# Chunked attention and a gated feed-forward on one core: first q through two hardware queues, moved groups from pair 6, paced loads, alternating moves, annealed orders

## The chip, the cores and the metric

One core of a Trainium2 chip runs the whole kernel. The metric is the device time of one execution in microseconds (us). The profiled execution has a span, from first to last instruction, that is 1.9 us shorter than the median time (251.2 and 249.3 before; the kernel before was timed once more beside the changed one, hence 251.4 below). A KB in the views is 1024 bytes; MB and GB/s are of 1000.

## The reference, cut to what matters

```python
# q, k, v: (8 batches, 8 heads, 576 tokens, 64); attention inside chunks of 64 tokens
scores = scale * q_c @ k_c.T ; attn = softmax(scores) ; out = attn @ v_c
x = out.transpose(0, 2, 1, 3).reshape(4608, 512)
a = x @ w1 ; b = x @ w2              # 512 -> 1024
h = a * b @ w3                       # 1024 -> 1024
return h @ w_out                     # 1024 -> 512, float32
```

The kernel multiplies w3 and w_out once (64 matmuls) and so needs 448 + 288 + 64 matmuls of 512 columns and 256 of 256 columns besides attention.

## The kernel before

The tokens are 18 "pairs" of 256 tokens, two to a group. One string gives the order of all steps; each engine executes its share of them strictly in that order. The letters:

- q, k, v: loads from memory with a cast to bf16, issued by POOL; i, o, h: loads of weights.
- T: VectorE transposes q or k of a pair (from the tile qk to qkT). S: scores, TensorE. E: exp, ScalarE. P: probabilities times v, TensorE. N: normalise, VectorE. X: transpose of the result, VectorE.
- A, B: x @ w1 and x @ w2, TensorE. C: copy of the first out of PSUM, ScalarE. M: product, VectorE. V, W, Z: w3 @ w_out. O, Y, Q: output matmul, copy, store.
- G, H: moves, of q and k (G, from qkT to qkm) and of the normalised result (H, from xm to xt). As the kernel lays its data out, the transpose leaves blocks of 32 partitions, so for early pairs scores are made with 32 contraction rows (64 matmuls a pair, the form 32*64 in the views). For "moved" pairs, DMAs from SBUF to SBUF (the memory on the chip that the engines read) put two blocks side by side first and 32 matmuls (64*64) do.
- D: matmuls of zeros whose result is not used. New in the change, R: a half of the first q, loaded as f32 by a hardware queue (SyncE's or ScalarE's); K: its cast to bf16, ScalarE.

```python
def load(dst, src):
    return inorder(nc.gpsimd.dma_start(dst, src))

vbuf = [consts.tile([P, 2, H, VW], bf, name=f"vbuf{i}") for i in range(6)]

def do_G(g, a):                       # moves of q and k of group g, 4 of 8
    if a == 0:
        qkm_t[g] = asb.tile([P, 2, 2, 2, H, CH], bf, tag="qkm", bufs=2, name="qkm")
    for i in (2 * a, 2 * a + 1):
        for e in range(2):
            move(qkm_t[g][blk[2 * a + e], i % 2], qkT_t[g][blk[i], e])

def do_S(p, hh=None):
    ...
        if p < 8:                     # 64 matmuls, 32 rows each
            ...
        else:                         # 32 matmuls, 64 rows each, from qkm
            ...

def do_M(p, j):
    if g not in ab_t:
        ab_t[g] = msb.tile([P, FO, GT], bf, tag="ab", bufs=3, name="ab")
    ...
# (cut: the other steps, and the order string)
```

The softmax here doesn't subtract the row's maximum and nothing guards it: scores larger than these inputs give would overflow.

## Time and profile before

| | before |
|---|---|
| median time | 251.2 us |
| span | 249.3 us |
| TensorE work at full rate (ledger of the prediction) | 217.8 us |
| lost until TensorE is dense (28.2 us) | 20.9 us |
| lost between there and the last matmul | 5.6 us |
| after the last matmul | 5.0 us |

In this profile, idle time counts only on the engine that sets the end. Here that is TensorE: it is full from 28 us on. So I read every other engine, and every transfer, by one question: does it make TensorE wait. The prediction below shows the lines.

### The profile page before, as it was taken

What the parts mean: (1) busy time and instruction counts of PE and PEld (TensorE: products, weight loads), DVE (VectorE), ACT (ScalarE), POOL (GpSimd) and SP (SyncE); (2) the same over time, 40 slices, a digit from 0 to 9 for tenths busy, and PEclk for the clock granted to TensorE, in tenths of its full rate; (3) what the DMA queues carried; (4) which work ended last, traced back from release to release, by engine and by line L of the source; (5) the groups of instructions that cost most, each with busy time, mean ns of one, the idle gap of its engine ahead of it and who ended that gap; (6) DMA issues with size and microseconds to landing.
All of it is one profiled execution on the core that took longest, in us unless ns stands there. A gap on an engine that the chain in (4) does not pass through costs nothing.

```text
span 249.3 us, 6372 instructions
## 1 busy us (share of the span) xinstructions
PE 226.9 (91%) x2740; PEld 122.0 (49%) x2760; DVE 154.5 (62%) x236; ACT 83.4 (33%) x116; POOL 86.9 (35%) x116
## 2 busy tenths in 40 slices
PE   3328899999999999999999999999999999999992
PEld 2225688874455445444444444444444444444441
DVE  2566965899879588999998798918440331233000
ACT  2110324332343333535335325262332332331322
POOL 8977854486997254573660000000000000000000
PEclk9999999999999999999999999999999999999998
DMA  7999999999999999999999974635502200400334
GB/s 67 145 165 182 193 185 201 196 174 172 155 169 209 221 225 249 177 209 193 204 194 235 271 128 99 147 76 199 151 3 84 84 0 9 162 0 1 139 116 168
DMA packets 93660, 37.12 MB, mean 149 GB/s; under 512 B 77120, under 2 KB 86592, under 8 KB 93632
## 3 DMA queue, kind: packets, MB, share of 16 engines
q0 software_dynamic: 84736, 19.41, 84.6%
q1 hardware_dynamic: 8896, 17.31, 24.0%
q8 instruction: 22, 0.36, 0.6%
q14 instruction: 6, 0.05, 0.1%
HBM read 38.80 MB, written 9.44 MB: 194 GB/s over the span
## 4 chain that ended last, share of the span: by engine, by line
PE 73%; DMA 17%; POOL 3%; DVE 2%; issue 1%; ACT 1%; SPq 0%; DVEq 0%; ACTq 0%; POOLq 0%
PE ab_ps L93 41%; PE o_ps L93 22%; DMA out_dram<-o_sb 6%; DMA w<-in_moe_w_dram 6%; PE w_ps L93 6%; DMA qkm<-qkT 5%; PE s_ps L93 3%; PE pv L93 2%; POOL qk L96 2%; DVE qkT L177 1%; POOL vbuf L96 1%; ACT e L209 0%; DVE ab L321 0%; POOL w L96 0%; ACT a_sb L306 0%
## 5 line engine op out<-in xcount | busy, mean ns | idle before, releaser
L93 PE MATMUL ab_ps<-xt,w 128*128 128x512 bf16 (+1 forms) x697 | 130.0, 343 | 1.1 <-DMA w<-in_moe_w_dram 0.5
L93 PEld LDWEIGHTS <-w 128*128 128x128 bf16 x704 | 67.8, 99 | 55.6 <-DMA w<-in_moe_w_dram 0.9
L321 DVE TENSOR_TENSOR ab<-a_sb,ab_ps 128x512 bf16<-128x512 f32 x72 | 48.9, 679 | 49.3 <-ACT a_sb L306 49.2
L306 ACT COPY a_sb<-ab_ps 128x512 f32<-128x512 f32 x72 | 42.2, 585 | 87.9 <-PE ab_ps L93 85.9
L93 PE MATMUL o_ps<-w3o,ab 128*128 128x512 bf16 (+1 forms) x285 | 63.3, 373 | 0.6
L177 DVE STREAM_TRANSPOSE qkT<-qk 128x1024 bf16<-128x1024 bf16 (+1 forms) x40 | 45.6, 1178 | 11.0 <-DMA qk<-in_q_dram 8.3
L93 PEld LDWEIGHTS <-ab 128*128 128x128 bf16 x296 | 28.5, 98 | 32.2
L96 POOL DMA_DIRECT2D vbuf<-in_v_dram x40 | 33.8, 854 | 14.6 <-DMA qk<-in_q_dram 6.4
L351 ACT COPY o_sb<-o_ps 128x1024 f32<-128x1024 f32 x17 | 17.2, 1012 | 42.8 <-PE o_ps L93 38.8
L239 DVE TENSOR_TENSOR xn<-pv,rc 128x512 bf16<-128x512 f32 x36 | 24.9, 692 | 1.2
L96 POOL DMA_DIRECT2D qk<-in_k_dram x26 | 20.2, 782 | 10.0 <-DMA vbuf<-in_v_dram 7.3
L96 POOL DMA_DIRECT2D qk<-in_q_dram x26 | 20.3, 788 | 8.2 <-DMA qk<-in_k_dram 2.3
L209 ACT ACTIVATE e<-s_ps 128x1024 bf16<-128x1024 f32 (+1 forms) x18 | 17.1, 978 | 8.9 <-PE s_ps L93 8.7
L93 PE MATMUL pv<-vbuf,e 64*32 64x65 bf16 (+1 forms) x832 | 11.0, 200 | 4.5 <-DMA vbuf<-in_v_dram 3.3
L93 PE MATMUL w_ps<-wo,w3T 128*128 128x512 bf16 x62 | 14.0, 379 | 0.1
L93 PEld LDWEIGHTS <-e 64*32 64x32 bf16 (+1 forms) x832 | 8.3, 99 | 11.5 <-issue 6.6
L236 DVE RECIPROCAL rc<-pv 128x8 f32<-128x8 f32 x36 | 6.9, 192 | 11.3 <-PE pv L93 11.2
L96 POOL DMA_DIRECT2D w<-in_moe_w_dram x16 | 11.1, 696 | 7.4 <-DMA wo<-in_moe_w_out_dram 3.4
L259 DVE STREAM_TRANSPOSE xm<-xn 128x512 bf16<-128x512 bf16 x20 | 13.6, 697 | 0.2
L251 DVE STREAM_TRANSPOSE xt<-xn 128x512 bf16<-128x512 bf16 x16 | 11.3, 707 | 0.4
L93 PEld LDWEIGHTS <-qkT 32*64 32x64 bf16 x512 | 5.8, 116 | 11.2 <-DVE qkT L177 9.2
L344 DVE COPY o_sb<-o_ps 128x256 f32<-128x256 f32 x1 | 0.4, 424 | 16.0 <-PE o_ps L93 16.0
(19 smaller groups left out, 45.4 us busy)
## 6 DMA issues: line engine op xcount, KB each, us to landing
out_dram<-o_sb SPq DMA_DIRECT2D x17, 512.0 KB, 2.9
qkm<-qkT SPq DMA_DIRECT2D x40, 128.0 KB, 7.2
vbuf<-in_v_dram POOLq DMA_DIRECT2D x32, 128.0 KB, 8.7
w<-in_moe_w_dram POOLq DMA_DIRECT2D x16, 256.0 KB, 10.0
qk<-in_q_dram POOLq DMA_DIRECT2D x10, 256.0 KB, 8.3
qk<-in_k_dram POOLq DMA_DIRECT2D x10, 256.0 KB, 10.1
xt<-xm SPq DMA_DIRECT2D x40, 64.0 KB, 3.0
qk<-in_q_dram POOLq DMA_DIRECT2D x8, 128.0 KB, 5.1
```

The lines of the kernel that those rows point to most:

```text
L93: return inorder(nc.tensor.matmul(*a, **kw))
L96: return inorder(nc.gpsimd.dma_start(dst, src))
L177: inorder(nc.vector.transpose(qkT_t[g][:, :, p % 2, s, heads(h)].rearrange("p e h (y t) -> p h t e y", t=2), qk_t[p][:, s, heads(h)].rearr ...
L209: inorder(nc.scalar.activation(e_t[p][:, :, heads(hh)], s_t[p][:].rearrange("p u (h q) -> p u h q", q=CH)[:, :, heads(hh)], Exp, scale=sca ...
L236: inorder(nc.vector.reciprocal(rc[:], pv[:, :, :, D:W]))
L239: inorder(nc.vector.tensor_mul(xn_t[p][:, u], pv[:, :, :, 0:D], rc.to_broadcast([P, 2, 4, D])))
L251: inorder(nc.vector.transpose(new_xt(g)[:].rearrange("p (o t) -> p o t", o=KO)[:, :, t0:t0 + UT] .rearrange("p o (m y) -> p m o y", y=BL), ...
L259: inorder(nc.vector.transpose(xm_t[g][:, u, :, m].rearrange("p o (c y) -> p c o y", y=BL), xn_t[p][:].rearrange("p u r m d -> p (u r) m d" ...
L306: inorder(nc.scalar.copy(a_t[p, j][:], ps_t[p, j][:, 0, :]))
L321: inorder(nc.vector.tensor_mul(o, view(a_t.pop((p, j))[:]), view(ps_t.pop((p, j))[:, 1, :])))
L344: inorder(copy(o_sb[:, u, n0:n1], t[:, 0, 0:n1 - n0]))
L351: inorder(nc.scalar.copy(o_sb[:], ps_t.pop(p)[:]))
```

## The change

Its intent: start TensorE earlier, save small matmuls in two more pairs, keep the loads from crowding the moves (three in flight), spread the moves over the blocks, and a new order of all steps found by annealing (a random search).

```diff
-q0.0 k0.0 q0.1 k0.1 v0 q1.0 q1.1 k1.0 k1.1 i0 v1 q2 k2 i1 v2 i2 i3 q3 k3 v3 o h0 h1 q4 k4 v4
-D0.0.32.64 T0.0.0 T0.1.0 T0.0.1 S0.0 T0.1.1 q5 k5 v5 E0.0 S0.1 ...
+R0 R1 k0 v0 q1 k1 v1 i1 i0 q2 k2 v2 i2 i3 q3 k3 v3 h0 o h1 q4 k4 v4 K0 K1 T0.0 T0.1 q5 k5 v5 S0 E0
+T1.0 D2.0.0.1 P0 N0.0 T1.1 ...
 # (cut: the rest of both orders; the new one has G3, H3 and ends Y15 Q15 Y16 Q16 O17)
+    def load(dst, src, paced=False):
+        if paced:
+            inorder(nc.gpsimd.tensor_copy(tick[0:1], last[-3]))
+        ins = inorder(nc.gpsimd.dma_start(dst, src))
 ...
+def do_R(h):
+    raw_t[h] = msb.tile([P, HH, 2 * D], f32, tag="o_sb", name="raw")
+    inorder((nc.sync, nc.scalar)[h].dma_start(raw_t[h][:], q[0, heads(h), ...]))
+def do_K(h):
+    inorder(nc.scalar.copy(qk_t[0][:, 0, heads(h)], raw_t[h][:]))
 # q, k and v loads pass paced = (p >= 6)
-        for i in (2 * a, 2 * a + 1):
-            for e in range(2):
-                move(qkm_t[g][blk[2 * a + e], i % 2], qkT_t[g][blk[i], e])
+        for i in (0, 2, 1, 3):
+            e = (i + a) % 2
+            move(qkm_t[g][blk[i // 2 * 2 + e], i % 2], qkT_t[g][blk[i], e])
 # the same in do_H; p < 8 becomes p < 6 in S, P, X, M; vbuf 6 -> 7 tiles, ab 3 -> 4
```

The copy into `tick` reads one element of the load three before. POOL works in order, so the next load is not issued until that one has landed.

More of the change, by code (lines that the diff above doesn't have):

```diff
@@ L9 @@
 ORDER = """
-q0.0 k0.0 q0.1 k0.1 v0 q1.0 q1.1 k1.0 k1.1 i0 v1 q2 k2 i1 v2 i2 i3 q3 k3 v3 o h0 h1 q4 k4 v4
-D0.0.32.64 T0.0.0 T0.1.0 T0.0.1 S0.0 T0.1.1 q5 k5 v5 E0.0 S0.1 E0.1 P0.0 P0.1 T1.0.0 N0.0 T1.1.0
-T1.0.1 S1.0 T1.1.1 q6 k6 v6 E1.0 X0.0 S1.1 N0.1 X0.1 P1.0 E1.1 T2.0 A0.0 T2.1 q7 k7 B0.0 C0.0 P1.1
-v7 M0.0 A0.1 N1.0 B0.1 C0.1 X1.0 S2 N1.1 E2 M0.1 X1.1 P2 A1.0 N2.0 B1.0 X2.0 C1.0 A1.1 N2.1 B1.1
-M1.0 C1.1 X2.1 A2.0 M1.1 B2.0 C2.0 A2.1 M2.0 B2.1 T3.0 C2.1 A0.2 M2.1 B0.2 C0.2 T3.1 q8 k8 v8 A1.2
@@ L15 @@
-M0.2 B1.2 C1.2 S3 M1.2 A2.2 E3 B2.2 C2.2 P3 M2.2 A0.3 N3.0 B0.3 X3.0 C0.3 A1.3 N3.1 B1.3 M0.3 C1.3
-X3.1 A2.3 M1.3 B2.3 C2.3 A3.0 M2.3 B3.0 V0 C3.0 A3.1 M3.0 B3.1 V1 C3.1 A3.2 M3.1 B3.2 C3.2 V2 A3.3
-M3.2 B3.3 C3.3 V3 W0 M3.3 T4.0 W1 Z0 V4 V5 T4.1 q9 k9 v9 W2 Z1 V6 V7 T5.0 S4 Z2 W3 T5.1 q10 k10 E4
-T6.0 T6.1 P4 v10 q11 k11 Z3 S5 N4.0 O0 E5 X4.0 N4.1 X4.1 T7.0 O1 T7.1 Y0 Q0 T8.0 P5 v11 q12 k12 Y1
-S6 T8.1 O2 Q1 E6 N5.0 X5.0 N5.1 X5.1 O3 T9.0 T9.1 Y2 G4.0 P6 v12 q13 k13 A4.0 N6.0 B4.0 G4.1 Y3 X6.0
@@ L20 @@
-N6.1 C4.0 A4.1 X6.1 B4.1 C4.1 M4.0 Q2 S7 Q3 M4.1 A4.2 E7 T10.0 B4.2 C4.2 T10.1 P7 v13 q14 k14 A4.3
-M4.2 B4.3 N7.0 C4.3 A4.4 X7.0 M4.3 B4.4 C4.4 N7.1 A4.5 M4.4 B4.5 C4.5 X7.1 S8 M4.5 S9 E8 A4.6 T11.0
-B4.6 E9 T11.1 P8 v14 q15 k15 C4.6 A4.7 M4.6 G5.0 B4.7 C4.7 N8.0 A6.0 M4.7 B6.0 N8.1 C6.0 G5.1 A6.1
-X8.0 B6.1 M6.0 C6.1 X8.1 P9 v15 q16 k16 A6.2 M6.1 N9.0 B6.2 C6.2 N9.1 A6.3 M6.2 B6.3 C6.3 X9.0 A6.4
-M6.3 B6.4 C6.4 X9.1 A6.5 T12.0 H4.0 B6.5 C6.5 M6.4 A6.6 M6.5 B6.6 T12.1 H4.1 C6.6 S10 S11 M6.6 E10
@@ L25 @@
-A6.7 T13.0 B6.7 E11 P10 v16 q17 k17 T13.1 C6.7 O4 M6.7 G6.0 N10.0 N10.1 X10.0 G6.1 P11 v17 Y4 X10.1
-O5 N11.0 N11.1 Q4 X11.0 X11.1 T14.0 A8.0 H5.0 Y5 B8.0 T14.1 C8.0 A8.1 M8.0 B8.1 H5.1 C8.1 T15.0 A8.2
-B8.2 M8.1 C8.2 T15.1 Q5 A8.3 B8.3 C8.3 M8.2 G7.0 S12 M8.3 S13 E12 A8.4 T16.0 B8.4 E13 G7.1 P12 T16.1
-C8.4 A8.5 B8.5 M8.4 C8.5 N12.0 A8.6 M8.5 B8.6 C8.6 N12.1 A8.7 M8.6 B8.7 C8.7 X12.0 P13 M8.7 A10.0
-X12.1 B10.0 C10.0 N13.0 A10.1 M10.0 B10.1 N13.1 C10.1 A10.2 X13.0 B10.2 M10.1 C10.2 X13.1 S14 S15
@@ L30 @@
-M10.2 E14 A10.3 H6.0 T17.0 B10.3 E15 P14 T17.1 C10.3 A10.4 H6.1 M10.3 B10.4 C10.4 N14.0 A10.5 M10.4
-B10.5 G8.0 C10.5 N14.1 A10.6 M10.5 B10.6 C10.6 X14.0 P15 G8.1 X14.1 A10.7 M10.6 B10.7 N15.0 C10.7 O6
-N15.1 M10.7 X15.0 X15.1 H7.0 S16 Y6 S17 O7 E16 E17 H7.1 P16 Y7 O8 Q6 N16.0 Q7 N16.1 X16.0 X16.1 P17
-Y8 A12.0 N17.0 Q8 B12.0 N17.1 C12.0 A12.1 X17.0 B12.1 M12.0 C12.1 X17.1 A12.2 M12.1 H8.0 B12.2 C12.2
-A12.3 M12.2 B12.3 C12.3 H8.1 A12.4 M12.3 B12.4 C12.4 A12.5 M12.4 B12.5 C12.5 A12.6 M12.5 B12.6 C12.6
@@ L35 @@
-A12.7 M12.6 B12.7 C12.7 O9 M12.7 O10 Y9 Q9 A14.0 Y10 B14.0 C14.0 Q10 A14.1 M14.0 B14.1 C14.1 A14.2
-M14.1 B14.2 C14.2 A14.3 M14.2 B14.3 C14.3 A14.4 M14.3 B14.4 C14.4 A14.5 M14.4 B14.5 C14.5 A14.6
-M14.5 B14.6 C14.6 A14.7 M14.6 B14.7 C14.7 O11 M14.7 O12 Y11 Q11 A16.0 Y12 B16.0 C16.0 Q12 A16.1
-M16.0 B16.1 C16.1 A16.2 M16.1 B16.2 C16.2 A16.3 M16.2 B16.3 C16.3 A16.4 M16.3 B16.4 C16.4 A16.5
-M16.4 B16.5 C16.5 A16.6 M16.5 B16.6 C16.6 A16.7 M16.6 B16.7 C16.7 O13 M16.7 O14 Y13 Q13 O15 Y14 Q14
-O16 Y15 Q15 O17 Y16 Q16 Y17 Q17
+R0 R1 k0 v0 q1 k1 v1 i1 i0 q2 k2 v2 i2 i3 q3 k3 v3 h0 o h1 q4 k4 v4 K0 K1 T0.0 T0.1 q5 k5 v5 S0 E0
@@ new lines @@
+T1.0 D2.0.0.1 P0 N0.0 T1.1 q6 k6 v6 N0.1 S1 X0.0 E1 X0.1 P1 A0.1 N1.0 X1.0 A0.0 N1.1 C0.1 T2.0 B0.1
+C0.0 X1.1 B0.0 T2.1 q7 k7 v7 A1.0 M0.1 S2 C1.0 M0.0 B1.0 E2 M1.0 P2 A1.2 N2.0 B1.2 X2.0 A0.2 N2.1
+A1.1 X2.1 C0.2 C1.2 B0.2 C1.1 A0.3 T3.0 B1.1 M1.2 M0.2 A2.0 T3.1 q8 k8 v8 C0.3 B2.0 C2.0 B0.3 M1.1
+S3 M0.3 A2.1 E3 M2.0 A1.3 C2.1 B2.1 C1.3 V0 P3 M2.1 B1.3 N3.0 A2.3 M1.3 B2.3 C2.3 V1 A2.2 V2 B2.2
+C2.2 W0 N3.1 X3.0 V3 X3.1 W1 M2.2 Z0 V4 M2.3 V5 A3.2 Z1 A3.1 T4.0 C3.2 B3.2 C3.1 T4.1 q9 k9 v9 A3.0
@@ new lines @@
+V6 B3.1 C3.0 S4 M3.2 B3.0 E4 T5.0 W2 M3.0 M3.1 V7 T5.1 q10 k10 v10 P4 Z2 W3 N4.0 T6.0 T6.1 q11 k11
+v11 S5 N4.1 Z3 A3.3 E5 T7.0 B3.3 C3.3 P5 T7.1 q12 k12 v12 O0 M3.3 G3.0 X4.0 N5.0 X4.1 G3.1 O1 N5.1
+Y0 X5.0 X5.1 Q0 T8.0 A4.0 T8.1 q13 k13 A4.1 C4.0 Y1 B4.0 T9.0 B4.1 C4.1 M4.0 S6 A4.2 M4.1 E6 T9.1
+B4.2 C4.2 P6 v13 q14 k14 M4.2 A4.4 G4.0 N6.0 A4.3 C4.4 T10.0 B4.4 C4.3 G4.1 O2 N6.1 T10.1 M4.4 Q1
+B4.3 Y2 T11.0 S7 A4.5 Q2 E7 M4.3 B4.5 C4.5 T11.1 P7 v14 q15 k15 A4.6 M4.5 G5.0 C4.6 N7.0 S8 B4.6 E8
+N7.1 S9 M4.6 G5.1 A4.7 E9 X6.0 P8 v15 q16 k16 C4.7 X6.1 B4.7 X7.0 O3 N8.0 H3.0 M4.7 X7.1 N8.1 H3.1
@@ new lines @@
+P9 v16 Y3 N9.0 S10 S11 X8.0 E10 O4 Q3 T12.0 E11 N9.1 X8.1 X9.0 P10 Y4 A6.3 H4.0 N10.0 B6.3 X9.1 C6.3
+A6.2 N10.1 B6.2 H4.1 M6.3 C6.2 P11 M6.2 A6.7 N11.0 A6.6 C6.7 T12.1 q17 k17 v17 B6.6 C6.6 B6.7 N11.1
+A6.1 M6.7 A6.0 M6.6 C6.1 T13.0 A6.4 B6.1 C6.4 T13.1 C6.0 B6.4 T14.0 G6.0 B6.0 O5 M6.4 M6.1 G6.1
+X10.0 X10.1 M6.0 A8.1 T14.1 B8.1 C8.1 X11.0 Y5 A8.0 M8.1 H5.0 B8.0 C8.0 A6.5 M8.0 A8.4 T15.0 C6.5 Q4
+B6.5 C8.4 S12 M6.5 S13 E12 B8.4 X11.1 A8.3 E13 H5.1 M8.4 B8.3 T15.1 C8.3 P12 A8.2 M8.3 G7.0 N12.0
@@ new lines @@
+B8.2 C8.2 N12.1 A8.7 M8.2 B8.7 C8.7 Q5 P13 G7.1 M8.7 A8.5 T16.0 A8.6 N13.0 B8.6 C8.6 C8.5 B8.5 N13.1
+A10.1 M8.5 A10.3 T16.1 B10.3 C10.3 M8.6 A10.0 M10.3 B10.0 X12.0 C10.0 C10.1 B10.1 M10.0 A10.2 M10.1
+B10.2 C10.2 T17.0 S14 S15 E14 A10.6 X12.1 M10.2 B10.6 E15 X13.0 A10.5 C10.6 H6.0 P15 M10.6 C10.5
+B10.5 T17.1 O6 N15.0 G8.0 M10.5 N15.1 G8.1 P14 Y6 A10.4 N14.0 B10.4 C10.4 A10.7 M10.4 O7 X13.1 C10.7
+N14.1 H6.1 X14.0 Q6 S16 B10.7 E16 O8 M10.7 Y7 X14.1 Q7 P16 Y8 A12.0 N16.0 B12.0 N16.1 C12.0 A12.1
@@ new lines @@
+X15.0 A12.6 M12.0 H7.0 C12.1 X15.1 A12.5 C12.6 B12.1 C12.5 S17 H7.1 M12.1 B12.6 A12.7 M12.6 B12.5
+C12.7 Q8 E17 B12.7 M12.5 O9 M12.7 A14.6 B14.6 C14.6 Y9 A14.2 M14.6 B14.2 Q9 A14.5 B14.5 C14.5 A14.0
+M14.5 B14.0 C14.0 C14.2 O10 M14.2 X16.0 M14.0 P17 Y10 A14.3 N17.0 B14.3 X16.1 C14.3 A12.3 N17.1
+A12.2 M14.3 A12.4 C12.2 C12.3 B12.3 A14.1 M12.3 B12.2 B12.4 M12.2 A14.4 B14.1 C14.4 C12.4 B14.4
+M12.4 O11 X17.0 X17.1 H8.0 O12 Y11 Q10 H8.1 C14.1 M14.1 M14.4 Q11 A14.7 B14.7 C14.7 Y12 O13 M14.7
+Q12 A16.3 A16.0 C16.3 Y13 B16.3 A16.6 C16.0 Q13 M16.3 B16.0 A16.5 M16.0 A16.1 C16.5 C16.6 B16.5
@@ L41 @@
+B16.6 M16.5 O14 M16.6 A16.7 Y14 B16.1 C16.1 Q14 A16.4 C16.7 M16.1 B16.4 C16.4 A16.2 B16.2 C16.2
+B16.7 M16.2 O15 M16.7 M16.4 O16 Y15 Q15 Y16 Q16 O17
 """
@@ L93, in mm @@
         return inorder(nc.tensor.matmul(*a, **kw))
-    def load(dst, src):
-        return inorder(nc.gpsimd.dma_start(dst, src))
+    last = []
+    tick = consts.tile([P, 1], bf, name="tick")
+    def load(dst, src, paced=False):
+        if paced:
+            inorder(nc.gpsimd.tensor_copy(tick[0:1], last[-3]))
+        ins = inorder(nc.gpsimd.dma_start(dst, src))
+        d = dst[0:1]
+        while len(d.shape) > 2:
+            d = d[:, 0]
+        last.append(d[:, 0:1])
+        return ins
     def psum(name):
@@ L110 @@
     inorder(nc.vector.memset(zero[:], 0.0))
-    vbuf = [consts.tile([P, 2, H, VW], bf, name=f"vbuf{i}") for i in range(6)]
+    vbuf = [consts.tile([P, 2, H, VW], bf, name=f"vbuf{i}") for i in range(7)]
     for t in vbuf:
@@ L128 @@
     HH = H // 2
+    raw_t = {}
+    def do_R(h):
+        raw_t[h] = msb.tile([P, HH, 2 * D], f32, tag="o_sb", name="raw")
+        inorder((nc.sync, nc.scalar)[h].dma_start(
+            raw_t[h][:], q[0, heads(h), 0:4 * CH, :].rearrange("h (p t) d -> p h (t d)", t=2)))
+    def do_K(h):
+        if 0 not in qk_t:
+            qk_t[0] = io.tile([P, 2, H, 2 * D], bf, tag="qk", bufs=5, name="qk")
+        inorder(nc.scalar.copy(qk_t[0][:, 0, heads(h)], raw_t[h][:]))
     def heads(h):
@@ L138, in load_qk @@
                 load(qk_t[p][at * BL:(at + m) * BL, s, heads(h)],
-                     (q, k)[s][b, heads(h), c * CH:(c + m) * CH, :].rearrange("h (p t) d -> p h (t d)", t=2))
+                     (q, k)[s][b, heads(h), c * CH:(c + m) * CH, :].rearrange("h (p t) d -> p h (t d)", t=2),
+                     p >= 6)
     def load_v(p):
@@ L143, in load_v @@
             for at, b, c, m in spans(4 * p + 2 * u, 2):
-                load(vbuf[p % 6][at * CH:(at + m) * CH, u, :, 0:D],
-                     v[b, :, c * CH:(c + m) * CH, :].rearrange("h p d -> p h d"))
+                load(vbuf[p % 7][at * CH:(at + m) * CH, u, :, 0:D],
+                     v[b, :, c * CH:(c + m) * CH, :].rearrange("h p d -> p h d"), p >= 6)
     def load_w(dst, ap, n0, n1):
@@ L193, in do_S @@
         for h in range(H)[heads(hh)]:
-            if p < 8:
+            if p < 6:
                 for e in range(2):
@@ L221, in do_P @@
             for m in range(4):
-                if p < 8:
+                if p < 6:
                     for g in range(NB) if hh is None else (2 * hh, 2 * hh + 1):
@@ L226, in do_P @@
                                lhsT=e[half[r], u, 2 * g + m % 2, m // 2 * BL:(m // 2 + 1) * BL],
-                               rhs=vbuf[p % 6][half[r], u, 2 * g + m % 2, 0:W], start=True, stop=True)
+                               rhs=vbuf[p % 7][half[r], u, 2 * g + m % 2, 0:W], start=True, stop=True)
                 else:
@@ L230, in do_P @@
                         mm(pv[half[g], r, m * W:(m + 1) * W], lhsT=e[half[r], u, 4 * g + m, :],
-                           rhs=vbuf[p % 6][half[r], u, 4 * g + m, 0:W], start=True, stop=True)
+                           rhs=vbuf[p % 7][half[r], u, 4 * g + m, 0:W], start=True, stop=True)
     def do_N(p, u):
@@ L248, in do_X @@
         g, m = divmod(p, 2)
-        if p < 8:
+        if p < 6:
             t0 = m * PT + u * UT
@@ L266, in do_H, with do_D @@
         xt = new_xt(g)[:].rearrange("p (s c) -> p s c", s=2)
-        for k_ in range(2):
-            for i in (2 * a, 2 * a + 1):
-                move(xt[blk[2 * a + k_], i % 2], xm_t[g][blk[i], k_].rearrange("p o m t -> p (o m t)"))
+        for i in (0, 2, 1, 3):
+            move(xt[blk[i // 2 * 2 + a], i % 2], xm_t[g][blk[i], a].rearrange("p o m t -> p (o m t)"))
     ab_t, ps_t, a_t, o_t = {}, {}, {}, {}
-    def do_D(which, p, n, cols):
-        d, key = (s_t, p) if which == 0 else (ps_t, (p, 0))
+    def do_D(which, p, j, n):
+        d, key = ((s_t, p), (ps_t, (p, j)), (pv_t, (p, 0)))[which]
         if key not in d:
@@ L278, in do_D @@
         for _ in range(n):
-            mm(d[key][:, 0, 0:cols], lhsT=zero[:, 0:P], rhs=zero[:, 0:cols], start=True, stop=True)
+            mm(d[key][:, 0, :], lhsT=zero[:, 0:P], rhs=zero[:], start=True, stop=True)
     def do_AB(p, j, f, which):
-        if p >= 8:
+        if p >= 6:
             rhs = new_xt(p // 2)[:].rearrange("p (s o t) -> p o s t", s=2, o=KO)
@@ L310, in do_M @@
         if g not in ab_t:
-            ab_t[g] = msb.tile([P, FO, GT], bf, tag="ab", bufs=3, name="ab")
+            ab_t[g] = msb.tile([P, FO, GT], bf, tag="ab", bufs=4, name="ab")
         if p < 4:
@@ L314, in do_M @@
             view = lambda t: t.rearrange("p (j t) -> p j t", j=2)
-        elif p < 8:
+        elif p < 6:
             o = ab_t[g][:, j]
@@ L390, in load_half3 @@
         load_w3(i * n, (i + 1) * n)
-    do = {"q": load_q, "k": load_k, "v": load_v, "i": load_w12, "o": load_wo, "h": load_half3, "T": do_T, "S": do_S, "E": do_E, "G": do_G, "H": do_H,
+    do = {"q": load_q, "k": load_k, "v": load_v, "i": load_w12, "o": load_wo, "h": load_half3, "T": do_T, "S": do_S, "R": do_R, "K": do_K, "E": do_E, "G": do_G, "H": do_H,
           "P": do_P, "N": do_N, "X": do_X, "A": do_A, "B": do_B, "C": do_C, "M": do_M, "D": do_D, "V": do_V,
```

## The prediction

> **What bounds the kernel now.** I read the page first, then the table of windows, then TensorE's instructions in order of time, then the moves and the last stores.
>
> From the page, busy tenths in 40 slices of 6.2 us:
>
> ```profile
> PE   3328899999999999999999999999999999999992
> ...
> DVE  2566965899879588999998798918440331233000
> ...
> DMA  7999999999999999999999974635502200400334
> ```
>
> TensorE is full from slice 5 to the last but one, idle at the start; the DMA engines are full from slice 1 to 22. So TensorE's work sets the time, and the loads set when it can begin. The windows (length, then busy us of PE, PEld, DVE, ACT, POOL, then clock, DMA share, GB/s):
>
> ```profile
> 0.00:5.00 5.00, 1.89 (x32) 1.73 (x32) 1.06 (x8) 1.28 (x1) 3.96 (x9) 1.00 0.56 53
> 5.00:10.00 5.00, 1.62 (x80) 1.31 (x81) 2.55 (x4) 1.19 (x2) 5.00 (x8) 1.00 1.64 132
> 10.00:15.00 5.00, 1.25 (x80) 1.04 (x79) 2.87 (x6) 0.00 (x0) 4.58 (x7) 1.00 1.49 160
> 15.00:20.00 5.00, 1.99 (x75) 1.52 (x68) 2.64 (x5) 1.19 (x2) 3.18 (x5) 1.00 1.95 171
> 20.00:25.00 5.00, 4.51 (x59) 3.11 (x58) 3.89 (x5) 0.58 (x1) 3.99 (x7) 1.00 1.78 182
> ...
> 130.00:150.00 20.00, 19.20 (x266) 9.32 (x265) 17.19 (x27) 8.10 (x13) 0.00 (x0) 1.00 1.25 210
> ...
> 225.00:249.30 24.30, 19.20 (x96) 9.33 (x96) 1.80 (x3) 6.08 (x8) 0.00 (x0) 0.96 0.29 109
> ```
>
> POOL is busy 3.96 to 5.00 of 5 us while the transfers reach only 53 and 132 GB/s: in the first 10 us the issuing engine holds the transfers back, afterwards the transfers themselves. TensorE in order of time:
>
> ```profile
> 7.12 0.64 PE L93 MATMUL z_ps<-qkT 32*64 32x64 bf16 x32 [4.04 <-DVE qkT L177]
> ...
> 14.44 0.64 PE L93 MATMUL s_ps<-qkT 32*64 32x64 bf16 x32 [3.22 <-DVE qkT L177]
> ...
> 19.48 3.28 PE L93 MATMUL ab_ps<-xt,w 128*128 128x256 bf16 x16
> ...
> 28.18 11.10 PE L93 MATMUL ab_ps<-xt,w 128*128 128x256 bf16 x96
> ...
> 148.96 0.93 PE L93 MATMUL s_ps<-qkm 64*64 64x64 bf16 x63 [0.41 <-DMA qkm<-qkT]
> ```
>
> It waits for transposed q and k, and is dense only from 28.18. The 16 matmuls at 19.48 take 205 ns each, those of a dense stretch 109 ns (112 from 42.33 to 54.57).
>
> **A ledger.** From starts in that view: a 512-column matmul 0.2158 us (64 from 192.33 to 206.14), a 256-column one 0.1093, scores of an unmoved pair 0.64, of a moved pair 0.32 (64 for two pairs, 99.09 to 99.73), probabilities times v 0.63 (93.18 to 93.81) and 0.38 (101.56 to 101.94). Work: 448 + 288 + 64 = 800 wide ones, 172.6; 256 narrow ones, 28.0; scores 8x0.64 + 10x0.32 = 8.3; pv 8x0.63 + 10x0.38 = 8.8. Sum 217.8 us. At 28.18 it had done three pairs of attention and 32 narrow matmuls, 3x1.27 + 3.5 = 7.3, so 20.9 us were lost by then. The last matmul ends at 244.3, which is 26.5 more than the work, so 5.6 us are lost later; 5.0 us follow as a tail. 217.8 + 20.9 + 5.6 + 5.0 = 249.3.
>
> **What the Trainium skill says.** (1) "DMA: Bandwidth & Descriptors", SWDGE vs HWDGE vs iDMA: a DMA that casts can only be issued from GpSimd. That is why the new q goes in as f32 and ScalarE casts it. The page's Specifications give about 1 us to the first byte from GpSimd and 0.6 us from sync or scalar. The trace here only has the former: the quickest q load landed 3.4 us after its issue began. (2) Same page, "Issuing engines are not separate DMA queues": all share 16 engines, so more queues save issue time only. The trace agrees in part: issue was short for 10 us, and only that can be won. (3) "SBUF — State Buffer", "Door 1: The DMA port swizzle": partition bit 6 picks even or odd ports, so partitions 0 to 63 reach half of 16. The old moves of one call stayed in one such half at the source and the destination; alternating blocks 0, 2, 1, 3 uses both. No run yet shows its worth. (4) "TensorE: Matmul & The Clock Gate", Part 1: an array idle for some 3.4 us runs at half rate until it was busy as long. The 205 against 109 ns agree, although the granted clock reads 1.00.
>
> **The change part by part.**
> *First q by two queues.* POOL issued q0, k0, v0, q1, k1 in 10 pieces of some 0.8 us before the first weights (9.0 us). Now it has k0, v0, q1, k1, v1 in 7, at 0.9 us, and q0 runs beside. It also moves first loads from 128 to 256 KB each. Both orders need the same 3.75 MB up to the third weight quarter, when TensorE can stay dense. Adding the windows (53x5, 132x5, ... KB), before moved 0.93 MB by 10 us, 3.49 MB by 25, and 3.75 MB at about 26.3. At 165 GB/s from 2.5 us on it would be 1.24 MB by 10 us: 0.31 MB more, 1.9 us earlier, so 24.4. The first quarter landed at 16.96, 1.8 us after that count (1.75 MB) said; so 26.2. Pair 0 itself wins little: it is no longer done in halves, and two casts of some 0.6 us come in. By then the new order has put 48 narrow matmuls (5.2) and three pairs (3.8) ahead of the wait, not 32. Allowing for the half rate, dense work starts at about 27, with 9.0 done: 18.0 lost instead of 20.9. Gain 2.9.
> *Pairs 6 and 7 moved.* 2x(0.32 + 0.25) = 1.1 us of TensorE, all on the path. It adds 8 moves of 128 KB and 8 of 64 KB, hidden if they land in time.
> *Pacing and alternating moves.* Each POOL load from pair 6 on first copies one element of the load three before. That costs POOL little (idle after 130 us). The moves of q and k took 7.2 us while loads ran and 2.4 us after they had ended:
>
> ```profile
> L169 SPq DMA_DIRECT2D qkm<-qkT x6: 591/593/606, 84.9 to 88.1; - x6
> DMA to landing us min/median/max: 6.9/7.2/7.6
> ...
> L169 SPq DMA_DIRECT2D qkm<-qkT x8: 512/586/597, 153.8 to 158.4; - x8
> DMA to landing us min/median/max: 2.3/2.4/2.4
> ```
>
> With three loads in flight, not about eight, I expect 4 to 5 us. TensorE's waits on moves were only 0.7 us in all; most of the 5.6 us is 0.1 us here and there at changes of operation. I take 1.1 us: 4.5 left.
> *The end of the order.* The last but one output is now copied and stored before the last one. Formerly its 512 KB store was issued behind three smaller ones:
>
> ```profile
> 243.74 1.02 ACT L351 COPY o_sb<-o_ps 128x1024 f32<-128x1024 f32 x1
> 244.40 0.42 DVE L344 COPY o_sb<-o_ps 128x256 f32<-128x256 f32 x1 [16.04 <-PE o_ps L93]
> ```
>
> A 512 KB store lands in 2.9 us, a 128 KB one in 1.8, and the issue of the big one (0.4 us) goes: 1.5 us. Tail 3.5.
> Sum: 2.9 + 1.1 + 1.1 + 1.5 = 6.6. Span 249.3 - 1.1 = 216.7 work + 18.0 + 4.5 + 3.5 = 242.7 us. The median time was 251.2 for a span of 249.3, so 1.9 more: 244.6 us, 2.6% less.
>
> **Rivals.**
> *The pacing starves attention.* Three loads of some 190 KB at about 4.4 us each (3.4 for the smallest, more for 256 KB) give 130 GB/s; unpaced loads had 150 between 55 and 85 us (4.49 MB in 30 us). The new order brings the scores of pairs 10 and 11 from 93 to 80 us of work, at about 18 + 80 + 1.5 = 99 us. Paced loads begin near 57 us; k of pair 11 is 4.25 MB later: 90 us at 130 GB/s. Two transposes (2.6) and a move (5) make it 97. Two us are left. At 105 GB/s, the loads' rate beside the moves in 85 to 110 us, it is 97.5 and TensorE waits 6 us: about 251, nothing gained.
> *The start is bound by the transfers anyway.* q0 takes its share of the same engines, and its f32 tile is twice the bytes written. Then k0 comes no earlier, and of 2.9 us perhaps 1 is left: 246.5. For it: 90% busy from slice 1. Against: 53 and 132 GB/s at first.
> *VectorE becomes the bound.* It is busy 14.2 and 14.5 of 15 us between 100 and 130. The new order asks it for pairs 8 to 11 earlier, and waits for w3 in line between. A wait there stalls every later step; 2 to 4 us, 247 to 249. Against: the last pairs' attention now comes later than before, so the crowded stretch is spread.
> *The annealed order closes more.* If the 5.6 us shrink to 2, 242.
>
> **Range and chances.** The parts that rest on counted work and the tail (2.6) are nearly sure; start and middle (4.0) can go to 0 or to 7. Predicted 244.6 us, 8 in 10 between 241 and 249.5. Faster by over 2% means under 246.2: a gain of 5.0, so 2.4 of the 4.0 less certain, 0.62. Within 2%: 0.34. Slower by over 2% needs a stall of over 10 us: 0.04.
>
> **What would show it.** Start: the first dense stretch begins near 27 us with 9 us of work done (18 lost), transfers above 132 GB/s in 5 to 10 us. Moved pairs: 128 fewer small matmuls, scores of pair 6 in 32. Pacing: q and k moves land in 4 to 5 us; no wait of TensorE above 1 us between 60 and 110. Tail: 3.5 us after the last matmul. Wrong if scores of pairs 6 to 11 wait on qkm, if TensorE's later losses exceed 6 us, or if the dense stretch begins after 28 us with no more done.

## The result, and the profile after

The changed kernel took 279.6 us (278.7 to 279.7, 4 runs) against 251.4, 11% more: ratio 1.112, 95% interval 1.105 to 1.119. A ratio is the mean time of one kernel's fast runs over that of the other's in the same rounds, so not quite the ratio of the medians. Executions over 1.5% slower than the fastest of the same kernel are left out of the means. The prediction of 244.6 us, range 241 to 249.5, was wrong, and in the wrong direction.

The page of the kernel after, busy tenths in 40 slices of 6.9 us:

```profile
PE   0378996999974795377999997899999999999994
...
DVE  3758739979392542487689676785351354113120
...
PEclk9999997999998598569999999999999999999999
DMA  9999999999999999899999999986522200622224
```

TensorE falls to 3 to 7 tenths in slices 12 to 19 (76 to 132 us; one slice has 9), and VectorE to 2 to 5 in slices 13 to 17: no compute engine is the busy one there, all of them wait. The DMA row stays at 8 or 9 all the while, although the windows below show fewer GB/s: it tells that transfers are under way, not how much they move. TensorE's granted clock drops in slices 13 to 18. By windows (the same columns as in the prediction), first before, then after:

```profile
85.00:100.00 15.00, 14.32 (x307) 7.18 (x309) 12.01 (x20) 5.77 (x9) 7.45 (x10) 1.00 1.61 226
100.00:115.00 15.00, 14.84 (x128) 6.88 (x130) 14.23 (x23) 6.00 (x10) 8.41 (x11) 1.00 1.74 194
```

```profile
55.00:70.00 15.00, 14.89 (x259) 9.52 (x262) 12.82 (x15) 4.99 (x7) 6.32 (x16) 1.00 1.17 95
70.00:85.00 15.00, 12.87 (x165) 6.68 (x153) 8.54 (x13) 4.75 (x6) 7.90 (x15) 1.00 1.26 134
85.00:100.00 15.00, 9.85 (x88) 4.31 (x88) 6.34 (x8) 3.36 (x5) 7.31 (x14) 0.66 1.28 157
100.00:115.00 15.00, 7.83 (x75) 3.34 (x75) 5.73 (x7) 2.62 (x3) 5.37 (x13) 0.79 1.11 191
115.00:130.00 15.00, 11.57 (x175) 5.49 (x176) 10.09 (x20) 4.12 (x5) 5.82 (x11) 0.76 1.24 161
```

Transfers fall to 95 GB/s in 55 to 70 us, where the kernel before had 164. What POOL and VectorE waited for in the kernel after (us in all, times, longest):

```profile
DVE qkT L200 <- DMA qk<-in_q_dram: 24.6, 9, 5.3
...
POOL tick L100 <- DMA qk<-in_k_dram: 20.8, 12, 4.6
POOL tick L100 <- DMA qk<-in_q_dram: 19.8, 11, 3.9
POOL tick L100 <- DMA vbuf<-in_v_dram: 14.1, 11, 2.6
```

POOL stood 55 us in its pacing copies. The chain of waits of the kernel after shows a link of it: a load lands, the copy runs, the next load is issued and takes its time (start, us, what):

```profile
77.59 9.57 DMA qk<-in_k_dram
87.20 0.08 issue
87.28 0.18 POOL tick L100
87.45 0.28 issue
87.73 5.31 DMA qk<-in_q_dram
```

The late load then reaches TensorE through VectorE. VectorE in order of time, kernel after:

```profile
113.20 1.31 DVE L200 STREAM_TRANSPOSE qkT<-qk 128x1024 bf16<-128x1024 bf16 x1 [5.32 <-DMA qk<-in_q_dram]
114.41 0.65 DVE L344 TENSOR_TENSOR ab<-a_sb,ab_ps 128x512 bf16<-128x512 f32 x1
...
117.00 1.31 DVE L200 STREAM_TRANSPOSE qkT<-qk 128x1024 bf16<-128x1024 bf16 x1 [1.94 <-DMA qk<-in_k_dram]
```

The product at 114.41 had its inputs from 104.2 us on (the end of its matmuls), but stands in line behind the transpose of a q that had not landed. It frees a PSUM tile, so TensorE waits "for a product" where the cause is a load. TensorE in order of time, kernel after:

```profile
26.67 6.29 PE L92 MATMUL ab_ps<-xt,w 128*128 128x256 bf16 x56
...
88.45 0.23 PE L92 MATMUL s_ps<-qkm 64*64 64x64 bf16 x1 [2.77 <-DMA qkm<-qkT]
...
107.94 2.94 PE L92 MATMUL ab_ps<-xt,w 128*128 128x512 bf16 x7 [3.35 <-DVE ab L344]
...
115.11 0.44 PE L92 MATMUL pv<-vbuf,e 64*64 64x65 bf16 x16 [3.88 <-DVE ab L344]
...
263.71 10.54 PE L92 MATMUL o_ps<-w3o,ab 128*128 128x512 bf16 x55
```

The first and last lines are the parts that went as predicted. The 7 wide matmuls at 107.94 take 2.94 us, 0.42 each, where a dense stretch has 0.2158: after the wait the array runs at half that rate, in a window whose granted clock was 0.79, so a wait costs more than its length.

**The ledger** (as in the prediction: work from durations and counts; start = begin of the dense stretch less the work done by then; tail = span less the end of the last matmul; middle = the rest):

| | work | lost at start | lost in the middle | tail | span |
|---|---|---|---|---|---|
| before | 217.8 | 20.9 | 5.6 | 5.0 | 249.3 |
| predicted | 216.7 | 18.0 | 4.5 | 3.5 | 242.7 |
| after | 216.6 | 17.6 | 40.0 | 3.5 | 277.7 |

Three terms came out to within 0.4 us. The whole error is the middle.

### The profile page after: what moved, and what is told of

It is laid out like the page before. It is cut to its first block, busy times and chain, and to the rows that moved or that the text cites. A ratio compares the mean times of both kernels' runs of the same rounds, so it can differ in the third digit from the quotient of the medians.

```text
span 277.7 us, 6183 instructions
## 1 busy us (share of the span) xinstructions
PE 233.4 (84%) x2580; PEld 121.9 (44%) x2601; DVE 152.9 (55%) x233; ACT 82.5 (30%) x116; POOL 93.0 (33%) x170
## 4 chain that ended last, share of the span: by engine, by line
PE 44%; DMA 38%; POOL 5%; DVE 5%; issue 4%; ACT 1%; SPq 1%; DVEq 0%; POOLq 0%
PE ab_ps L92 24%; PE o_ps L92 16%; DMA w<-in_moe_w_dram 11%; DMA qk<-in_q_dram 10%; DMA vbuf<-in_v_dram 7%; DMA qk<-in_k_dram 7%; DVE qkT L200 3%; DMA qkm<-qkT 2%; PE w_ps L92 2%; POOL qk L101 2%; POOL w L101 2%; DVE ab L344 1%; POOL vbuf L101 1%; DMA xt<-xm 1%; ACT a_sb L329 1%
## 5 line engine op out<-in xcount | busy, mean ns | idle before, releaser
L92 PE MATMUL ab_ps<-xt,w 128*128 128x512 bf16 (+1 forms) x699 | 139.6, 355 | 12.4 <-DVE ab L344 6.5
L200 DVE STREAM_TRANSPOSE qkT<-qk 128x1024 bf16<-128x1024 bf16 x36 | 46.3, 1301 | 37.8 <-DMA qk<-in_q_dram 24.6
L374 ACT COPY o_sb<-o_ps 128x1024 f32<-128x1024 f32 x17 | 17.2, 1014 | 38.4 <-PE o_ps L92 34.7
L233 ACT ACTIVATE e<-s_ps 128x1024 bf16<-128x1024 f32 x18 | 18.1, 1024 | 23.9 <-PE s_ps L92 23.9
L101 POOL DMA_DIRECT2D qk<-in_q_dram x23 | 17.8, 776 | 6.9 <-issue 2.2
L100 POOL COPY tick<-qk 1x1 bf16<-1x1 bf16 x32 | 5.7, 177 | 41.0 <-DMA qk<-in_k_dram 20.8
L92 PE MATMUL pv<-vbuf,e 64*64 64x65 bf16 (+1 forms) x736 | 10.4, 204 | 7.5 <-DVE ab L344 5.2
L283 DVE STREAM_TRANSPOSE xm<-xn 128x512 bf16<-128x512 bf16 x24 | 16.3, 693 | 0.0
L92 PE MATMUL s_ps<-qkT 32*64 32x64 bf16 x384 | 5.0, 207 | 10.5 <-DVE qkT L200 10.3
L92 PE MATMUL s_ps<-qkm 64*64 64x64 bf16 x384 | 6.7, 206 | 7.0 <-DMA qkm<-qkT 3.6
L385 DVE STREAM_TRANSPOSE w3T<-w 128x1024 bf16<-128x1024 bf16 x8 | 9.7, 1225 | 4.8 <-DMA w<-in_moe_w_dram 4.8
## 6 DMA issues: line engine op xcount, KB each, us to landing
w<-in_moe_w_dram POOLq DMA_DIRECT2D x16, 256.0 KB, 9.8
qk<-in_k_dram POOLq DMA_DIRECT2D x12, 256.0 KB, 7.2
qk<-in_q_dram POOLq DMA_DIRECT2D x11, 256.0 KB, 5.3
wo<-in_moe_w_out_dram POOLq DMA_DIRECT2D x4, 256.0 KB, 11.0
```

The source lines that it names most:

```text
L92: return inorder(nc.tensor.matmul(*a, **kw))
L100: inorder(nc.gpsimd.tensor_copy(tick[0:1], last[-3]))
L101: ins = inorder(nc.gpsimd.dma_start(dst, src))
L200: inorder(nc.vector.transpose(qkT_t[g][:, :, p % 2, s, heads(h)].rearrange("p e h (y t) -> p h t e y", t=2), qk_t[p][:, s, heads(h)].rearr ...
L233: inorder(nc.scalar.activation(e_t[p][:, :, heads(hh)], s_t[p][:].rearrange("p u (h q) -> p u h q", q=CH)[:, :, heads(hh)], Exp, scale=sca ...
L283: inorder(nc.vector.transpose(xm_t[g][:, u, :, m].rearrange("p o (c y) -> p c o y", y=BL), xn_t[p][:].rearrange("p u r m d -> p (u r) m d" ...
```

## The experiments

The theory after the result: pacing at three loads starves attention, and an in-order VectorE passes each late load on to TensorE. The rival: the new order stalls by itself, or the earlier moved groups crowd the transfers.

**e1_unpaced: the change without its pacing copies**

```diff
-        if paced:
-            inorder(nc.gpsimd.tensor_copy(tick[0:1], last[-3]))
```

> The changed kernel without its pacing copies; all else stays. Theory 'pacing starves': with 3 loads in flight POOL waited 55 us for landings and loads moved 95 GB/s in 55 to 70 us where before had 164, so q and k of pairs 8 to 11 came 20 to 40 us late; without pacing the time falls to 243 to 249 us and TensorE's waits between 70 and 135 us nearly vanish. Rival 'the order itself': the new order puts transposes of pairs not yet loaded ahead of VectorE's products, and would stall even with loads at full rate: 255 to 270 us. Rival 'moves of pairs 6 and 7 crowd the loads': also above 255.

Measured: 264.1 us (262.9 to 265.2), ratio 1.052 [1.044, 1.059]. Pacing cost 15.5 us (279.6 less 264.1), but 13 us over the kernel before stayed. By the ranges the theory missed and the rivals' were hit; by the size, neither alone was right. Ledger (work + start + middle + tail): 216.6 + 18.1 + 25.2 + 3.5.

The load of k of pair 11 shows a part of why. Its second part, before: issue and time to landing, then the transpose of pair 11 (second of the two in the last line, at about 101.7):

```profile
L96 POOL DMA_DIRECT2D qk<-in_k_dram x1: 769/769/769, 82.4 to 82.4; - x1
...
DMA to landing us min/median/max: 13.9/13.9/13.9
...
100.42 2.49 DVE L177 STREAM_TRANSPOSE qkT<-qk 128x1024 bf16<-128x1024 bf16 x2
```

The same in e1:

```profile
L99 POOL DMA_DIRECT2D qk<-in_k_dram x1: 769/769/769, 83.1 to 83.1; - x1
...
DMA to landing us min/median/max: 15.2/15.2/15.2
...
98.38 1.30 DVE L198 STREAM_TRANSPOSE qkT<-qk 128x1024 bf16<-128x1024 bf16 x1 [1.46 <-DMA qk<-in_k_dram]
```

Before, it landed at 82.4 + 13.9 = 96.3 and was used 5 us later: slack. In e1 it landed at 98.3, no earlier, and VectorE stood waiting for it. In the changed kernel it was issued at 112.96 and landed 4.0 us later, at 117.0, the transpose shown above at 117.00. With the early moves in it, the new order wants these pairs earlier than even unpaced loads deliver them.

**e2_six: six loads in flight**

```diff
-            inorder(nc.gpsimd.tensor_copy(tick[0:1], last[-3]))
+            inorder(nc.gpsimd.tensor_copy(tick[0:1], last[-6]))
```

> Six loads in flight in place of three. Theory 'pacing starves': most of the loss returns, as six loads of 190 KB in 6 to 7 us give about 165 GB/s, near the unpaced rate: 244 to 253 us. If the copies themselves (POOL waiting, then 0.3 us of issue after each) are the cost rather than the depth: still 270 or more. Rival 'order itself': same as e1, 255 to 270.

Measured: 265.4 us (263.1 to 266.1, and one slow run of 268.5), ratio 1.055 [1.047, 1.064]: the same as e1. My range for it missed, as it did not know of the other 13 us. But the step from three to six gives back 14 of the 15.5 us of pacing, with the copies still in. It is the depth that costs, not the copies.

**e3_before_paced: the kernel before with the same pacing**

```diff
+        if paced:
+            inorder(nc.gpsimd.tensor_copy(tick[0:1], last[-3]))
 # and p >= 6 passed by the loads of q, k and v
```

> The kernel before with the same pacing of loads from pair 6 on, nothing else changed. Theory 'pacing starves': the old order has more slack (k of pair 11 landed near 77 us and its scores ran at 116), but loads at about 80 GB/s need until some 175 us for pair 17, which the old order uses at 163: 262 to 280 us. Rival 'order itself': pacing costs the old order little, under 255 us.

Measured: 287.9 us (287.0 to 288.5, and one slow run of 292.9), ratio 1.147 [1.139, 1.154]; 37 us more than before, above my range. The slack was smaller than I had counted on: I wrote that k of pair 11 had landed near 77 us, and the lines above have it at 96.3. Its last load of k was issued at 176.05 us against 126.50 without pacing; in the changed kernel it was 176.68. Pacing harms either order. Why the old order suffers more was not tried.

**e4_before_tail: the kernel before with only the new end**

```diff
-O16 Y15 Q15 O17 Y16 Q16 Y17 Q17
+O16 Y15 Q15 Y16 Q16 O17 Y17 Q17
```

> The kernel before with the last but one output copied and stored ahead of the last one's matmuls, as in the new order. Prediction's term: 1.5 us less, about 249.7 us, the span's end 3.5 us after the last matmul, not 5.0. Rival: the end is set by the last small stores and their completion anyway: within 0.4 us.

Measured: 249.3 us (249.2 to 251.2), ratio 0.996 [0.990, 1.002]: by time alone unclear, as the interval holds 1. The trace shows the term itself: the last matmul ends at 226.51 + 17.45 = 243.96, the span at 247.4, so a tail of 3.4 us instead of 5.0.

**e5_before_start: the kernel before with only the new start**

```diff
-q0.0 k0.0 q0.1 k0.1 v0 q1.0 q1.1 k1.0 k1.1 i0 v1 q2 k2 i1 v2 i2 i3 ...
+R0 R1 k0 v0 q1 k1 v1 i0 i1 q2 k2 v2 i2 i3 ... K0 K1 T0.0 T0.1 q5 k5 v5 S0 E0 T1.0 P0 ...
 # (cut: first three pairs rewritten to match; do_R and do_K added)
```

> The kernel before with only the new start: q0 by two hardware queues and ScalarE casts, whole-pair loads, and the first three pairs' order rewritten to match; moved groups, moves and pacing as before. In e1 the new start left 18.1 us lost at 27.2 us, as predicted, against 20.9 before. Theory 'start gains its 2.9 us': 247 to 249 us, dense work near 27 us. Rival 'the start's gain is given back at the next wait for weights or loads': 250 to 252 us.

Measured: 248.7 us (247.9 to 248.9), ratio 0.989 [0.983, 0.996], 2.4 us less. Dense from 28.0 us with 10.8 us of work done: 17.2 lost instead of 20.9.

**e6_new_no_loads and e7_before_no_loads: no loads from pair 6 on**

```diff
+        if p >= 6:
+            qk_t[p] = qk_t[1 + (p - 1) % 5]
+            return
 # load_v returns for p >= 6 as well; e6 is built on e1, e7 on the kernel before
```

> Wrong result on purpose: the unpaced new order (e1) with no loads of q, k, v from pair 6 on; those pairs compute on the tiles of pairs 1 to 5. Takes away both the waits for late loads and their traffic beside moves and stores. Theory 'the new order needs loads and moves to land sooner than they do': 242 to 249 us, the loss between 80 and 135 us (15 us in e1) falls to under 4, q and k moves land in 2.4 us. Rival 'the order stalls by itself, on VectorE or on PSUM tiles': above 255 us.

> Control, wrong result on purpose: the kernel before with the same loads taken out. Its waits on loads and moves after 30 us were under 2 us in all, so 247 to 250 us: little to gain. If it gains 5 us or more, the old order was bound by transfers too and e6 says less.

Measured: e6 251.3 us (249.4 to 252.4), ratio 1.000 [0.992, 1.007]; e7 250.2 us (249.2 to 251.7), ratio 0.997 [0.989, 1.004]. Their outputs are wrong, which doesn't matter for the times. Without the loads the new order's middle shrinks from 25.2 to 9.6 us (216.6 + 17.9 + 9.6 + 3.3 = 247.4), and TensorE has no wait for a load or a move left; the old order gains 2.2 us in the middle (e7: 217.8 + 20.1 + 3.4 + 5.3 = 246.6). So the new order suffers from the loads' traffic and the old one hardly does. But e6 missed my 242 to 249: with loads for nothing the new order would only equal the old one. It keeps waits of its own, such as these for a PSUM tile that ScalarE had still to copy out:

```profile
140.56 5.34 PE L92 MATMUL ab_ps<-xt,w 128*128 128x512 bf16 x24 [1.16 <-ACT a_sb L332]
147.07 2.75 PE L92 MATMUL ab_ps<-xt,w 128*128 128x512 bf16 x12 [1.16 <-ACT a_sb L332]
```

The moves of q and k between 60 and 100 us, first e6 (alternating), then e7 (old order of moves):

```profile
L195 SPq DMA_DIRECT2D qkm<-qkT x24: 507/589/1911, 68.3 to 96.5; - x24
...
DMA to landing us min/median/max: 2.3/2.4/4.1
```

```profile
L174 SPq DMA_DIRECT2D qkm<-qkT x8: 586/592/599, 82.9 to 87.3; - x8
...
DMA to landing us min/median/max: 2.4/2.4/2.5
```

2.4 us in both: what stretches them to some 7 us is the loads.

**e8_w3_later: the unpaced new order with w3's transposes behind the products**

```diff
-... C1.3 V0 P3 M2.1 B1.3 N3.0 A2.3 M1.3 B2.3 C2.3 V1 A2.2 V2 B2.2 C2.2 W0 ... V3 X3.1 W1 ...
+... C1.3 P3 M2.1 B1.3 N3.0 A2.3 M1.3 B2.3 C2.3 N3.1 X3.0 A2.2 X3.1 B2.2 C2.2 M2.3 M2.2 V0 ...
```

> The unpaced new order with the transposes of w3 moved some 4 us later on VectorE, behind the products of the third pairs, which they held up in e1 while w3 was still on its way (3.8 us of VectorE wait, TensorE idle 2.0 us and then at half rate for 32 matmuls). Theory 'in-order VectorE passes a late load on to TensorE': 3 to 4 us less than e1, 260 to 261 us. Rival 'the wait only moves to the next step': within 1 us of e1, 263 to 265.

Measured: 263.2 us (262.8 to 263.6), ratio 1.048 [1.042, 1.054]: within 1 us of e1. Here are the scores of pair 5 and, 50 us on, the first matmuls of pair 6's gated layer, e1 first, then e8:

```profile
69.11 0.71 PE L92 MATMUL s_ps<-qkT 32*64 32x64 bf16 x64
...
119.40 6.52 PE L92 MATMUL ab_ps<-xt,w 128*128 128x512 bf16 x16 [2.94 <-DMA out_dram<-o_sb]
```

```profile
64.39 0.70 PE L92 MATMUL s_ps<-qkT 32*64 32x64 bf16 x64
...
118.27 3.61 PE L92 MATMUL ab_ps<-xt,w 128*128 128x512 bf16 x16 [2.71 <-DMA out_dram<-o_sb]
```

TensorE came 4.7 us sooner to pair 5 and 1.1 us sooner to pair 6: the gain was given back, as the rival said, to waits for later transfers. The store named in the last lines is not the one waited for: in e1 it landed at 120.4, after the matmuls had begun. They read xt, and the last recorded move of pairs 6 and 7 to xt landed at 118.7 (issue 111.2, 7.5 us). A releaser's name can be wrong where several semaphores are waited for.

**e9_before_alternate: the kernel before with only the alternating moves**

```diff
-        for i in (2 * a, 2 * a + 1):
-            for e in range(2):
+        for i in (0, 2, 1, 3):
+            e = (i + a) % 2
 # targets as in the change; do_H likewise
```

> The kernel before with only the moves' order changed to alternate between the blocks; no pacing, old order. Without loads the moves landed in 2.4 us in both orders (e6, e7), so the blocks are not what limits a single move. Theory 'moves wait for the loads in the same engines': landing stays 7 to 8 us between 85 and 130 us and the time stays within 1 us of before. Rival 'alternating spreads the ports': landing falls under 6 us; the time still hardly moves, as TensorE waited only 0.7 us for moves.

Measured: 249.7 us (248.6 to 250.1), ratio 0.995 [0.992, 0.999]. The q and k moves between 85 and 110 us still landed in 7.2 us in the median, as before. Those between 110 and 135 us did land sooner, first before, then e9:

```profile
DMA to landing us min/median/max: 7.0/8.1/8.3
```

```profile
DMA to landing us min/median/max: 5.6/6.5/8.0
```

TensorE's waits on qkm, 0.7 us before, are gone from the list. So alternating helps a part of the moves, for a small gain in time. Why not those of 85 to 110 us is not shown.

**e10_start_tail: new start and new end on the kernel before**

```diff
 # e5's start and e4's end
```

> The two parts that worked, together: the new start (e5, 2.4 us less) and the tail (e4, 1.4 us less). If independent: 3.5 to 4 us less than before, 246.5 to 247.5 us, ratio near 0.985. If the earlier start only moves TensorE's waits into the middle: 248 to 249.

Measured: 247.0 us (245.7 to 247.7), ratio 0.985 [0.982, 0.989]. The two add up.

**e11_start_tail_moved6: e10 with moved groups from pair 6**

```diff
-            if p < 8:
+            if p < 6:
 # in S, P, X, M, and p >= 6 in A, B; the order gets
-T7.1 Y0 Q0 T8.0 P5 v11 q12 k12 Y1 S6 T8.1 ... X7.1 S8 ...
+T7.1 G3.0 G3.1 Y0 Q0 T8.0 P5 v11 q12 k12 Y1 T8.1 ... O3 S6 ... X7.1 H3.0 M4.4 B4.5 C4.5 H3.1 S8 ...
 # and O4, O5 ahead of A6.0
```

> e10 with moved groups from pair 6, without pacing, and with the scores of pair 6 and the outputs of pairs 4 and 5 shifted so that the extra moves have 7 us to land. Theory 'moved pairs save 1.1 us if their moves are hidden': 245.5 to 246.5 us. Rival 'sixteen more moves in the crowded stretch delay loads and the moves of later pairs': 247 to 251 us, with waits on qkm or xt after 85 us.

Measured: 256.6 us (256.0 to 259.7), ratio 1.026 [1.021, 1.030]; 9.6 us more than e10. The rival was right in kind, and its 247 to 251 us too low. Its order also shifts three steps (in the diff), so not all of this need be the moves. TensorE's waits in e11:

```profile
PE s_ps L92 <- DMA qkm<-qkT: 3.7, 2, 2.5
PE ab_ps L92 <- DMA xt<-xm: 2.4, 1, 2.4
```

6.1 us on moves alone, against 0.2 in e10, for 1.1 us of matmuls saved. The middle loses 17.9 us (216.6 + 17.0 + 17.9 + 3.3 = 254.8). The loads suffer too: k of pair 11 landed at 100.9 us, against 94.1 in e10.

**e12_start_tail_alternate: e10 with the alternating moves**

```diff
 # e10 and e9's two loops
```

> e10 with the alternating order of moves. In e9 alternating took 1.1 us (ratio 0.995) off the old kernel though the moves' landing stayed at 7.3 us. If that adds to start and tail: 245.5 to 246.5 us, ratio 0.98. If not: 247 as e10.

Measured: 246.4 us (246.1 to 247.3), ratio 0.983 [0.979, 0.988]: ahead of both kernels. Against e10 the intervals overlap, so alternating is not shown to add, although the moves between 105 and 140 us landed in 6.8 us in the median here and in 7.9 in e10. TensorE on its page:

```profile
PE   0248999899999989999999999999999999999994
...
DMA  8999999999999999999999913736402200400244
```

No dip is left in the middle: 217.8 + 17.6 + 5.9 + 3.3 = 244.6.

**e13_new_moved8: the unpaced new order, moved groups from pair 8 again**

```diff
-                if p < 6:
+                if p < 8:
 # everywhere; G3.0 G3.1 H3.0 H3.1 taken out of the order
```

> The unpaced new order (e1) with moved groups from pair 8 again, as before; only the moves of pairs 6 and 7 are left out of the order. Theory 'the earlier moved groups are what the new order cannot feed' (they cost 9.6 us in the old order, e11 against e10): 253 to 257 us, and no wait on qkm before 95 us. Rival 'the annealed order asks for pairs 8 to 11 too early whatever pairs 6 and 7 do': 261 to 265.

Measured: 258.5 us (257.5 to 260.1), ratio 1.032 [1.026, 1.038], between the ranges of the two theories: 5.6 us of e1's excess went with the earlier moved groups. Ledger 217.8 + 17.7 + 16.5 + 3.3 = 255.3. The loads came sooner: the second part of k of pair 11, issued at 78.2, landed at 87.6 us, not 98.3, and from 30 us on VectorE waited only 0.5 us for q and k, where it had waited 4.7 us in e1:

```profile
L99 POOL DMA_DIRECT2D qk<-in_k_dram x1: 772/772/772, 78.2 to 78.2; - x1
...
DMA to landing us min/median/max: 9.4/9.4/9.4
...
DVE qkT L198 <- DMA qk<-in_q_dram: 0.5, 1, 0.5
```

But the run is not clean. VectorE has a wait that e1 has not (e13, VectorE in order of time):

```profile
90.64 1.32 DVE L198 STREAM_TRANSPOSE qkT<-qk 128x1024 bf16<-128x1024 bf16 x1 [6.46 <-PE s_ps L92]
```

This transpose, of q of pair 10, writes a qkT tile (there are two) that the scores of pair 7 still read in e13, as they are not moved. The next product in line, whose inputs were there at 85.3 us, ran at 93.9.

**Together.** 279.6 to 264.1: pacing, 15.5 us. 264.1 to 258.5: moved groups from pair 6, 5.6 us. 258.5 to the 246.4 of e12, which has the same start, tail and moves in the old order: 12 us for the annealed order and the deeper v and ab buffers. (By the ratios, which allow for the chip, the steps are 15, 5 and 12 us.) The second figure is net of the new wait in e13, and the third holds it. Loads that come too late are hardly in the third (0.5 us of waits, above). How much of it is that wait of 6.5 us on VectorE, how much slow moves and how much the order's own waits for PSUM tiles (1.16 us several times) was not separated.

## Why the prediction was right or wrong

- *The start*: right. 18.0 lost foretold, 17.6 to 18.1 measured in the new order; 2.4 us of time by itself (e5). The reasons held too: 163 to 166 GB/s instead of 132 in 5 to 10 us.
- *The end*: right, 3.5 us after the last matmul, 3.4 in e4.
- *Pairs 6 and 7 moved*: the 1.1 us of TensorE are there (216.6), but the condition "hidden if they land in time" was not examined. It fails. It costs 5.6 us net in the new order and 9.6 in the old one (e13, e11).
- *Pacing and alternating moves*: the step that failed. It gave pacing a gain (moves landing in 4 to 5 us) and left 4.5 us lost in the middle; it was 40.0, 15.5 us of it by the pacing alone (e1). The moves landed in 6.0 us in the median over the whole run, 4.4 to 7.5 between 70 and 190 us by window, so the gain was small. The loss was on the other side: q, k and v came later. Without pacing (e1) 25.2 us were still lost there, for which the sum has no term.
- *The rival "The pacing starves attention"* named the mechanism, and its size was wrong. It had three loads of 190 KB in flight at 4.4 us each, so 130 GB/s. Measured, from the first paced issue at 59.8 us to k of pair 11 at 117.0: 27 loads of 165,000 bytes in the mean, 4.46 MB (the prediction's 4.25 counts by 1024), so 78 GB/s. All three factors were less good: the pieces were smaller, 2.7 were in flight in the mean instead of 3, and they took 5.65 us in the mean instead of 4.4 (issue and landing times of the 23 whose landing is recorded). Until the first move at 77.4 us the loads did land in 2.4 to 5.2 us, and even then they came at 85 GB/s (1.57 MB from 59.8 to 78.2); beside moves and stores some took 9 to 10.6 us.
- *The unpaced rate*, reckoned in the same way: 102 GB/s in e1 (54.5 to 98.3 us), near the 105 that the rival named as its bad case, but 129 in e13 (53.2 to 87.6), where the moves of pairs 6 and 7 are not there. The prediction let the loads slow the moves, but had no cost for what the new moves do to the loads.
- *The rate should have warned*. A load's landing time under traffic was in the traces of before, 7 to 13 us in the median by stretch, with 5.7 in flight in the mean up to k of pair 11 (the prediction had "about eight"). To hold three of them to 4.4 us was a hope that the queueing was all their own; part of it was moves and stores.
- *The rival "VectorE becomes the bound"* was wrong as put (VectorE was less busy than before, 5.73 of 15 us in 100 to 115). But its last half sentence, that a wait in its line stalls every later step, is how the loss reached TensorE.
- *The order* was taken as neutral or better ("the annealed order closes more"). Even without loads it loses 9.6 us in the middle (e6), where the old order loses 3.4 (e7). I had compared the sums of work ahead of each score with my own load times, and those were too early: 90 us for k of pair 11 with pacing, where without pacing it landed at 98. A slip that changes nothing: "249.3 - 1.1 = 216.7 work" is meant as 217.8 - 1.1.

## What to carry to other kernels

Limiting loads in flight trades latency against rate (here 5.65 us a load and 78 GB/s with three, 9.5 us and 102 GB/s unpaced): before doing it, take the landing time under traffic from the trace, and check that depth times size over that time still meets the first deadline. When an engine works in order, read a wait for it as a wait for whatever stands at the head of its line; a late load ahead of a product holds the array. Apply a bundle of changes one at a time: here the start and the end were worth 1.5% together, and the whole bundle cost 11%.

## What the Trainium skill lacked or had wrong

- "DMA: Bandwidth & Descriptors", section "Anatomy of one DMA — SWDGE (gpsimd) path", fits a single DMA as 2.0 us + bytes / 436e3, so an estimate of 2.6 us for 256 KB. It has nothing on a casting load beside other traffic: with three in flight, loads of 256 KB took 5.0 to 7.4 us in the median by window between 70 and 100 us, the k shown 9.6. No page says how many must be in flight to keep the rate; here three gave 78 GB/s up to pair 11 and no pacing 102, and six took about the same time as no pacing (265.4 and 264.1 us).
- "SBUF — State Buffer", "Door 1: The DMA port swizzle" was not wrong: it speaks of the ports that the partitions of one transfer reach. That separate moves which alternate between the halves land faster was my own step from it, and the trace agrees in part: 6.5 us against 8.1 in the median between 110 and 135 us (e9 and before), no difference between 85 and 110 (7.2) or without loads (2.4 in e6 and e7), at 128 KB and 32 partitions each.
- No page has what a move within SBUF takes beside casting loads on the same engines: 6.5 to 8.1 us in the median by stretch (before and e9, 85 to 135 us) against 2.4 without them (e6, e7).
